# V of a sliding-window attention by dense products, one evacuation and SBUF-to-SBUF placement

## Chip, cores, metric

One core of one Trainium2 chip. The metric is device time in microseconds (us) of one execution. Kernels are compared only within the same rounds. All timed runs were fast but one, which is named.

## The reference

```python
h = layernorm(x) * (1 + ca) + sa            # x: 2048 x 512; ca, sa, ga, ... from c @ w_mod
q, k, v = split(h @ wqkv)                   # 32 heads of 16
scores = q k^T / 4, masked to 0 <= i - j < 256
x = x + ga * (softmax(scores) @ v @ wo)
h = layernorm(x) * (1 + cb) + sb
x = x + gb * (gelu(h^T @ w1 + b1) @ w2 + b2)^T   # token MLP, F = 1792
```

## The kernel before

The program is a list of about 1,380 small operations (`op`). `ORDER` says in which sequence they are put on the engines' instruction lists. It also names the engine where there is a choice: D for VectorE, A for ScalarE, P for GpSimd. Tokens are worked in four groups of 512, each of four blocks of 128 tokens. The attention runs in 75 chunks, E0 to E74. Each chunk has scores (S, TensorE into PSUM), two exponentials on ScalarE, a mask product, and products with V (AV, into `pxy`).

```python
def run_order(ops):
    for word in ORDER.split():        # "359D": operation 359, on VectorE
        n = int(word.rstrip("ADP")); o = ops[n]
        if any(d.n in left for d in o.deps): raise RuntimeError(o.name)
        left.discard(n); o.emit(...)
```

The V part of a block: 32-column tiles of TensorE put the tokens of the two 64-token halves where `VT` wants them. Two half-height casts bring them there. `VT` keeps zero columns beside every head, 16 columns of V and 16 of zeros, so it is cleared once.

```python
VT = [kvpool.tile([P, 8, DH, 2 * DH], BF, ...) for r in range(3)]   # group G uses VT[G % 3]
vt_zero = [[op("vz", ... memset(VT[r][:, 2*n : 2*n+2, :, :], 0.0)) for n in range(4)] for r in range(3)]

def v(tb, pos):                              # one block of 128 tokens
    for i in range(2):                       # two halves of 64 tokens
        for dc in range(ND):
            for q in range(4):
                te.matmul(pv[32*q : 32*(q+1), i, :], lhsT=h1T[:, dc, tok], rhs=wv[:, dc, q // 2, :, :],
                          tile_position=(0, 32 * q), ...)
    def e_ve(e, par):
        rows = slice(KB * par, KB * (par + 1))
        copy(e, VT[r3][rows, 2*tb : 2*tb+2, :, par*DH : (par+1)*DH], pv[rows, ...])
    bs = [op("ve", {"ACT": .53, "DVE": .62}, ...) for par in range(2)]
    v_done[G, tb] = bs
```

The softmax here doesn't subtract the row's maximum and nothing guards it: scores larger than these inputs give would overflow.

## Time and profile before

| | before |
|---|---|
| time, median (range) | 268.49 us (267.96 to 268.76, 3 runs) |
| start of the profile to the first exponential (E0) | 15.68 us |
| E0 to E74 | 171.10 us, ScalarE's gaps over 0.12 us sum to 5.1 (the 5.2 of the prediction takes in those from 0.10 on) |
| E74 to the end | 80.00 us |
| VectorE busy | 205.0 us |

ScalarE's row of 75 pairs of exponentials sets the time up to E74, and TensorE's products with w1 and w2 set it from there on. So three numbers tell a run: when E0 starts, how long E0 to E74 takes, and the tail. The lines behind this are in the prediction.

### The profile page before, as it was taken

The page shows a single profiled execution, that of the slowest core. Times are in us where ns is not written, and L with a number is a line of the kernel's source. Part 1 is how long each engine was busy: PE and PEld are TensorE (multiplying, and loading weights), DVE is VectorE, ACT ScalarE, POOL GpSimd, SP SyncE. Part 2 cuts the span into 40 slices and gives each one's busy share as a digit, 9 for nine tenths or more (in the row PEclk, how much of TensorE's full clock was granted, in tenths as well). Part 3 has the DMA queues.
Part 4 walks back from the last instruction along what each step waited for, and adds up shares of the span by engine and source line. Part 5 has one row for each costly group of instructions (what it writes and reads, how often), then busy time and mean ns, then how long its engine had stood idle before and what let it go on. Part 6 is the DMA issues. An engine that isn't in the chain of part 4 may idle for free.

```text
span 266.8 us, 10593 instructions
## 1 busy us (share of the span) xinstructions
PE 249.1 (93%) x4737; PEld 136.2 (51%) x4737; DVE 205.0 (77%) x439; ACT 186.6 (70%) x281; POOL 70.4 (26%) x146
## 2 busy tenths in 40 slices
PE   7799999999998996978999999999999999999993
PEld 2477655755666653644454544444534444444441
DVE  7588988879958589999946999999998640263585
ACT  3289999999998999998999999999613850000000
POOL 8667500624460781324920012010000000000000
PEclk9999999999999999999999999999999999999999
DMA  7999100002300005000090220035599600011122
GB/s 208 322 349 232 4 2 5 6 2 84 81 5 2 6 5 157 5 2 4 14 301 8 84 79 4 2 81 150 133 397 416 249 1 2 0 59 60 42 79 79
DMA packets 31446, 24.81 MB, mean 93 GB/s; under 512 B 6056, under 2 KB 29608, under 8 KB 31400
## 3 DMA queue, kind: packets, MB, share of 16 engines
q1 hardware_dynamic: 31392, 24.13, 29.8%
q8 instruction: 37, 0.61, 1.0%
q14 instruction: 9, 0.07, 0.1%
q10 hardware_dynamic: 8, 0.00, 0.0%
HBM read 22.03 MB, written 2.10 MB: 90 GB/s over the span
## 4 chain that ended last, share of the span: by engine, by line
PE 69%; DVE 14%; ACT 7%; DMA 5%; SPq 2%; issue 2%; DVEq 0%; ACTq 0%
PE pu L193 33%; PE pxy L193 10%; PE pq L193 9%; PE psa L193 9%; ACT et L193 5%; PE pa L193 4%; PE pv L193 3%; DVE VT L193 3%; DMA w<-in_B_w_dram 3%; DVE et L193 2%; DMA x<-in_A_x_dram 2%; DVE st L193 2%; SPq L193 2%; PE ps_b L193 1%; DVE h1T L193 1%
## 5 line engine op out<-in xcount | busy, mean ns | idle before, releaser
L193 ACT ACTIVATE et<-psa 128x1536 bf16<-128x1536 f32 x75 | 109.2, 1456 | 5.6 <-PE psa L193 2.6
L193 PE MATMUL pu<-hb,w1p 128*128 128x512 bf16 x224 | 54.6, 380 | 1.2 <-DVE part L193 0.5
L193 PE MATMUL pu<-guT,w 128*128 128x512 bf16 x224 | 49.2, 379 | 0.0
L193 ACT ACTIVATE et<-psb 128x512 bf16<-128x512 f32 x75 | 44.8, 601 | 0.0
L193 PE MATMUL pxy<-et,VT 128*32 128x192 bf16 (+3 forms) x960 | 37.7, 234 | 1.0 <-DVE OT L193 0.6
L193 PE MATMUL pxy<-et,ones_bd 128*32 128x192 bf16 (+3 forms) x960 | 37.9, 233 | 0.0
L193 PE MATMUL pq<-h1T,wqkv 128*128 128x512 bf16 (+1 forms) x160 | 34.1, 338 | 2.5 <-DVE kb L193 1.1
L193 PEld LDWEIGHTS <-w 128*128 128x128 bf16 x224 | 21.9, 98 | 26.4
L193 PE MATMUL psa<-QT,KT 32*128 32x192 bf16 (+3 forms) x720 | 30.0, 231 | 4.2 <-ACT et L193 3.5
L193 PEld LDWEIGHTS <-w1p 128*128 128x128 bf16 x224 | 20.0, 98 | 26.5 <-issue 4.0
L193 POOL TENSOR_SCALAR KT<-kb,mask_par 128x512 bf16<-128x512 bf16 (+1 forms) x36 | 24.1, 679 | 34.7 <-DVE kb L193 18.3
L193 DVE SCALAR_TENSOR_TENSOR o<-pu,b2FM,bc_gb 128x512 f32<-128x512 f32 x16 | 11.7, 748 | 25.2 <-PE pu L193 25.2
L193 PE MATMUL psb<-QT,KT 32*128 32x192 bf16 (+3 forms) x240 | 29.4, 231 | 0.0
L193 PEld LDWEIGHTS <-KT 32*128 32x128 bf16 x960 | 15.1, 92 | 26.8 <-issue 25.3
L193 PEld LDWEIGHTS <-VT 128*32 128x32 bf16 x960 | 23.3, 96 | 10.2 <-issue 8.7
L193 DVE TENSOR_TENSOR et<-et,maskt 128x512 bf16<-128x512 bf16 (+2 forms) x56 | 24.9, 479 | 0.5 <-ACT et L193 0.4
L193 PEld LDWEIGHTS <-ones_bd 128*32 128x32 bf16 x960 | 23.0, 97 | 0.1
L193 DVE BATCH_NORM_STATS2 st<-x 128x6 f32<-128x512 bf16 x32 | 21.9, 684 | 1.5 <-DMA x<-in_A_x_dram 1.3
L193 DVE CAST VT<-pv 64x512 bf16<-64x512 f32 x30 | 20.5, 686 | 3.0 <-PE pv L193 2.1
L193 PEld LDWEIGHTS <-wqkv 128*128 128x128 bf16 x160 | 13.4, 97 | 14.3 <-issue 4.9
L193 DVE TENSOR_TENSOR OT<-pxy,lz 128x256 bf16<-128x256 f32 x32 | 13.3, 415 | 9.5 <-ACT lz L193 9.4
L193 POOL TENSOR_SCALAR xn<-x,nm,rs 128x512 bf16<-128x512 bf16 x13 | 10.8, 834 | 32.2 <-DVE nm L193 22.6
(93 smaller groups left out, 347.5 us busy)
## 6 DMA issues: line engine op xcount, KB each, us to landing
w1p<-in_B_w_dram SPq DMA_DIRECT2D x14, 512.0 KB, 5.2
w<-in_B_w_dram SPq DMA_DIRECT2D x14, 512.0 KB, 10.1
wmod<-in_w_mod_dram SPq DMA_DIRECT2D x6, 512.0 KB, 6.6
x<-in_A_x_dram SPq DMA_DIRECT2D x16, 128.0 KB, 5.5
out_dram<-otile SPq DMA_DIRECT2D x16, 128.0 KB, 1.7
wqkv<-in_A_wqkv_dram SPq DMA_DIRECT2D x2, 384.0 KB, 6.2
wqkv<-in_A_wqkv_dram SPq DMA_DIRECT2D x1, 512.0 KB, 5.9
wod<-in_A_wo_dram SPq DMA_DIRECT2D x1, 512.0 KB, 8.9
```

Source lines behind the costliest of these rows:

```text
L193: ins = call(*args, **kwargs)
```

## The change

Intent: TensorE's products of V for groups 1 to 3 become dense (4 products of 512 columns per block in place of 32 small ones). A block is evacuated by one full-height cast into a small tile `VN` that has the zero columns already. Four SBUF-to-SBUF transfers of 64 KB (64 rows of 1 KB) put it into `VT`. Group 0 keeps the old way. The whole `ORDER` is new as well. The diff cut to its core (new list, names, and parts for another setting cut):

```diff
+VN_BUFS = 2
+VN = [kvpool.tile([P, 2, D + DH], BF, name=f"VN{r}") for r in range(VN_BUFS)]
-vt_zero = ... for r in range(3)
+vt_zero = ... VT[0] only;  vn_zero = [op("vz", ... memset(VN[n][:], 0.0)) for n in range(VN_BUFS)]
 def v(tb, pos):
+    te.matmul(box["v", tb][:], lhsT=h1T[:, dc, tb*P : (tb+1)*P], rhs=wqkv[:, dc, 2*D : 3*D], ...)
+    vr = len(v_placed) % VN_BUFS
+    copy(e, VN[vr][:, :, 0:D] ..., box["v", tb][:] ...)
+    b = op("ve", {"ACT": .495, "DVE": .6}, e_ve,
+           deps=[halves[1]] + (v_placed[-VN_BUFS] if len(v_placed) >= VN_BUFS else [vn_zero[vr]]))
+    for i in range(2):
+        for par in range(2):
+            sp.dma_start(out=VT[r3][KB*par : KB*(par+1), 2*tb + i, :, :] ...,
+                         in_=VN[vr][...][KB*i : KB*(i+1), D*par : D*(par+1)])
+            placed.append(op("vp", {"SP": .4}, e_vp, deps=[b] + war))
+    v_placed.append(placed); v_done[G, tb] = placed
```

Each `vp` is a word of its own in `ORDER`, and SyncE issues its transfers strictly in the order of the list.

## The prediction

> **What bounds the kernel now.** I read the page first, then the groups of instructions with shapes kept apart, then busy time by stage, then the order in time of ScalarE. The page says TensorE 93% busy, but the kernel has two regimes and only one of them is TensorE's.
>
> ```profile
> PE 249.1 (93%) x4737; PEld 136.2 (51%) x4737; DVE 205.0 (77%) x439; ACT 186.6 (70%) x281; POOL 70.4 (26%) x146
> ACT  3289999999998999998999999999613850000000
> L193 ACT ACTIVATE et<-psa 128x1536 bf16<-128x1536 f32 x75 | 109.2, 1456 | 5.6 <-PE psa L193 2.6
> L193 ACT ACTIVATE et<-psb 128x512 bf16<-128x512 f32 x75 | 44.8, 601 | 0.0
> ```
>
> The second line is ScalarE's busy tenths in 40 slices of 6.67 us: nearly all nines from slice 4 to slice 28, then little. Those are the 75 chunks of the attention, each with two exponentials. By stage (columns: stretch, length, busy us of PE, weight loads, DVE, ACT, POOL, clock, DMA share, GB/s):
>
> ```profile
> 64.00:96.00 32.00, 29.83 (x970) 19.38 (x959) 23.66 (x53) 30.81 (x47) 14.68 (x21) 1.00 0.08 20
> 96.00:128.00 32.00, 26.96 (x746) 16.39 (x744) 30.70 (x65) 30.44 (x43) 12.26 (x19) 1.00 0.14 36
> 128.00:160.00 32.00, 31.79 (x644) 15.72 (x648) 25.10 (x56) 31.17 (x44) 7.72 (x8) 1.00 0.39 101
> 189.00:266.80 77.80, 72.31 (x388) 32.47 (x386) 46.00 (x81) 14.37 (x30) 0.00 (x0) 1.00 0.33 123
> ```
>
> ScalarE is busy 30.4 to 31.2 us of every 32; between 96 and 128 us VectorE is just as full (30.7) while TensorE falls to 27.0. The last 77.8 us belong to TensorE. In the ScalarE timeline the first exponential starts at 15.68 us and the last at 186.78. Adding every gap of more than 0.12 us in front of a ScalarE instruction in between gives 5.2 us, 18 gaps, the two largest here:
>
> ```profile
> 14.96 0.82 ACT L193 ACTIVATE kb<-pq 128x256 bf16<-128x256 f32 x2 [1.05 <-PE pq L193]
> 15.68 1.44 ACT L193 ACTIVATE et<-psa 128x1536 bf16<-128x1536 f32 x1
> ...
> 84.45 1.45 ACT L193 ACTIVATE et<-psa 128x1536 bf16<-128x1536 f32 x1 [0.78 <-PE psa L193]
> ```
>
> (The other is 1.00 us at 124.93, waiting for psb.) So a change that touches neither the exponentials nor the last stage can win the start before 15.68 us and those 5.2 us, no more.
>
> **What the Trainium skill says.** "VectorE: DVE Perf Modes", section "Why `tensor_reduce` can't reduce along partition axis": the engine streams along the free dimension, every partition being its own lane. Then 64 partitions cost what 128 do, and the trace agrees: the first two rows below, 64x512 at 686 ns and 128x512 at 681. "TensorEngine Tiling (Array Packing)", "PSUM Bottleneck": tiling speeds up TensorE but not the evacuation. V before is such a case: its 32-column tiles put both heads of a pair in the right place, at two half-height evacuations per block. "DMA: Bandwidth & Descriptors", "Anatomy of one DMA": about 2 us fixed per transfer, given there for GpSimd's path; the nearest here, 128 KB stores on SyncE's queue, land in a median of 1.7 us.
>
> **The change, part by part.** These are the rows it acts on, from the groups by shape:
>
> ```profile
> L193 DVE CAST VT<-pv 64x512 bf16<-64x512 f32 x30 | 20.5, 686 | 3.0 <-PE pv L193 2.1 <-ACT VT L193 0.4
> L193 DVE CAST kb<-pq 128x512 bf16<-128x512 f32 x11 | 7.5, 681 | 0.1
> L193 POOL MEMSET VT<- 128x1024 bf16 x7 | 6.7, 952 | 0.1
> L193 DVE MEMSET VT<- 128x512 uint32 x5 | 2.4, 485 | 0.3
> L193 PE MATMUL pv<-wqkv,h1T 128*32 128x256 bf16 x512 | 17.1, 273 | 1.0 <-issue 0.4 <-DVE VT L193 0.4
> ```
>
> *Evacuations.* Groups 1 to 3 have 12 token blocks. 24 casts of 0.686 us (16.5 us) become 12 of 128x512 at about 0.68 (8.2): VectorE gives up 8.3 us.
>
> *Memsets.* The built program has 4 memsets of VT instead of 12, and 2 of the new tile VN: VectorE 5 to 3 (1.0 us less), GpSimd 7 to 3 (3.8 less). GpSimd is 26% busy, so that half is worth nothing directly.
>
> *TensorE.* 384 matmuls of 32x256 become 48 of 128x512. By durations this looks like a gift; it is not. The chain of waits shows 32 of the tiled ones, one block, in 0.87 us where nothing disturbs them (43.06), and four 512-column products of Q or K in 0.86 to 0.97. Four tiles side by side take a quarter of the time each. I book 0, though 672 fewer instructions stand in its queue.
>
> *What the new order moves.* The whole order of the program is a list, and it is a new one. Counting both built programs: VectorE takes over xn (3 x 0.42), kb (2 x 0.40 and 1 x 0.68), part (0.68), h1T (0.53 - 0.40), and gives up QT (0.41), h (0.42) and some small ones. That is about 2.7 us back, so VectorE's net is 8.3 + 1.0 - 2.7 = 6.6 us less. ScalarE between the first and last exponential loses h1T (0.77), kb (0.62), part (about 0.6), and gains h1T (0.56), KT (0.47), QT (0.39), a second evacuation of the first group's V inside chunk 0 and a pair of small rs (0.5); it had two such evacuations before too. Minus 2.0 plus 1.9: no change. **ScalarE's floor in the attention stays where it was.**
>
> *Start.* Before, ScalarE copies two kb tiles (14.96 to 15.78) ahead of the first exponential, although the first scores left TensorE at 14.4. In the new order these copies are VectorE's and come after it. Nothing then stands between: 14.4 to 14.5, 1.2 us earlier. h1T also comes ahead of a statistics pass that waited for x until 9.70, some tenths more. But VectorE then has about 11.8 us of work over the first five chunks (summed from the durations above), against 11.6 us that those took before; part of the lead is lost. I book 0.9.
>
> *Gaps.* Inside the critical stretch of 96 to 128 us there are 12 VT casts, 8.0 us, of which about half go. The 1.00 us gap at 124.93 lies right behind two such casts and a kb (122.48 to 124.5), and TensorE's queue waited for VT casts 7 times for 3.2 us in all. A block's PSUM buffer is now held for one cast, not two. I book 2.2 of the 5.2 us.
>
> *Transfers.* 48 of 64 KB, 64 rows of 1 KB. At 0.45 us per issue (14 w2 issues took 11.75 us with waits, x issues 0.42 to 0.46) that is 22 us of SyncE, idle otherwise between 25 us and the w1 loads. A block needs an evacuation (0.7), up to four issues (1.8) and a landing (about 1.7): 4.2 us, or two chunks of 2.3. In the built order the blocks of groups 2 and 3 precede their first use by at least four chunks; the tightest are the last three of group 1, two chunks ahead. I book 0.3 of new waits.
>
> *Last stage.* The same products stand behind the last exponential in both orders: 96 + 8 + 224. At 0.2165 us (250 in 54.13) that is 71.0 of its 77.8 us. One w1 load now follows three w2 loads, but about 44 products (9.5 us) precede its use. I book 0.
>
> Sum: 268.5 - 0.9 - 2.2 + 0.3 = 265.7.
>
> **The rivals.** *VectorE was the bound, so its whole 6.6 us come off:* for it, 30.7 of 32 us at 96 to 128; against, ScalarE has 30.4 in the same stretch and lost 1.2 us there. With the earlier start as well, and every gap closed, 261.5 to 262.5. *The transfers become the wait:* two VN tiles only, and a VN may be overwritten only when its four transfers have landed; some stand in SyncE's queue behind a 512 KB w1 load that takes 5.2 us to land. A late VectorE cast holds up what follows on that engine. For it, one such re-use within a chunk of its last transfer in group 3; against, VectorE has slack now. 267 to 270. *TensorE gains from 672 fewer instructions:* the weight loads show 49.2 us of "issue", so perhaps the queue limits it; then the gaps close faster, 264. Against: TensorE's idle time is in ScalarE's shadow.
>
> **Range and chances.** Best case 261.5, worst plausible 270; the parts that I book are each uncertain by about 1 us, and three executions of one kernel lay within 0.8. 8 in 10: 262.9 to 268.3. Faster by over 2% means under 263.1, nearly all gaps closed: 0.11. Slower by over 2%: 0.02.
>
> **What would show it.** Right if: ScalarE's first exponential starts at 14.0 to 14.8 us and its gaps up to the last sum to 2 to 4 us; VectorE's busy time falls by 5 to 8 us; a V block takes about 0.87 us of TensorE; the last stage keeps 77 to 78.5 us. Wrong if pxy products or VN casts wait for DMA by over 1 us in all, if a VN cast takes much over 0.7 us, or if the last stage moves by over 1 us.

## The result, and the profile after

| | before | after |
|---|---|---|
| time, median (range) | 268.23 us (267.73 to 268.76, 4 runs) | 269.63 us (269.24 to 269.73, 4 runs) |
| ratio | | 1.0049, 95% interval 1.0025 to 1.0073 |
| E0 / E15 in the profile | 15.68 / 52.41 us | 13.76 / 52.00 us |
| E15 to E74 | 134.37 us | 136.04 us |
| E74 to the end | 80.00 us | 79.49 us |

A ratio is the mean time of one kernel's fast runs over that of the other's of the same rounds, so not quite the ratio of the medians quoted. Later the same changed kernel had ratios of 1.0078 and 1.0032. I use the mean of the three, 1.0053, or +1.4 us, where I had predicted -2.8.

The prediction's own sign of failure ("wrong if pxy products or VN casts wait for DMA by over 1 us in all") is there: casts alone waited 3.7 us.

VectorE's relief came out exactly, and the casts cost what was said. From the page of the changed kernel, and from its groups by shape (columns: busy us, mean ns of one, idle before them and what ended it):

```profile
PE 244.8 (92%) x4355; PEld 131.9 (49%) x4401; DVE 198.4 (74%) x429; ACT 186.1 (70%) x278; POOL 63.7 (24%) x141
...
VT<-VN SPq DMA_DIRECT2D x48, 64.0 KB, 3.1
```

```profile
L195 DVE CAST VN<-pv 128x512 bf16<-128x512 f32 x12 | 8.3, 688 | 7.8 <-DMA VT<-VN 3.7 <-PE pv L195 2.2 <-PE psb L195 1.8
```

VectorE is at 198.4 us against 205.0: 6.6 less, as predicted. But the 12 casts stood idle 7.8 us, half of it for the transfers, and a transfer lands in a median of 3.1 us. The stretches that the prediction showed:

```profile
64.00:96.00 32.00, 29.14 (x876) 18.40 (x879) 22.89 (x51) 30.87 (x47) 11.58 (x20) 1.00 0.24 57
96.00:128.00 32.00, 25.88 (x600) 14.02 (x595) 29.16 (x67) 30.04 (x43) 12.49 (x16) 1.00 0.47 122
128.00:160.00 32.00, 31.51 (x600) 15.82 (x605) 23.65 (x53) 30.65 (x42) 4.23 (x6) 1.00 0.14 37
189.00:267.50 78.50, 72.30 (x408) 32.92 (x399) 47.12 (x83) 15.64 (x33) 0.00 (x0) 1.00 0.35 128
```

Between 96 and 128 us VectorE gave up 1.5 us, and ScalarE is no fuller than before (30.04 against 30.44). The relief is there and does not reach the engine that bounds.

The start, in ScalarE's timeline of the changed kernel (start, us, then what ran; brackets: idle before, and releaser):

```profile
13.76 1.45 ACT L195 ACTIVATE et<-psa 128x1536 bf16<-128x1536 f32 x1
15.11 0.59 ACT L195 ACTIVATE et<-psb 128x512 bf16<-128x512 f32 x1
15.59 0.30 ACT L195 ACTIVATE rs<-mv,eps_t 128x2 f32<-128x2 f32 x1
15.91 0.20 ACT L195 ACTIVATE rs<-rs 128x2 f32<-128x2 f32 x1
16.73 1.07 ACT L195 ACTIVATE VT<-pv 64x512 bf16<-64x512 f32 x2 [0.61 <-DVE VT L195]
17.70 1.44 ACT L195 ACTIVATE et<-psa 128x1536 bf16<-128x1536 f32 x1
19.03 0.59 ACT L195 ACTIVATE et<-psb 128x512 bf16<-128x512 f32 x1
20.11 0.56 ACT L195 ACTIVATE h1T<-pt,modFM 128x256 bf16<-128x256 bf16 x1 [0.49 <-PE pt L195]
```

E0 starts 1.92 us earlier, but work that stood ahead of E0 now stands between the first exponentials. ScalarE's work ahead of E0 is 2.7 us against 4.4 (one load of 1.28 us at the very beginning, the same in both, is left out). E4 starts at 26.36 against 24.79, later than before.

What the transfers did, from the timeline of the same run (VectorE, TensorE and ScalarE):

```profile
59.13 0.69 DVE L195 CAST VN<-pv 128x512 bf16<-128x512 f32 x1 [2.38 <-DMA VT<-VN]
...
62.49 0.69 DVE L195 CAST VN<-pv 128x512 bf16<-128x512 f32 x1 [1.28 <-DMA VT<-VN]
...
97.73 0.69 DVE L195 CAST VN<-pv 128x512 bf16<-128x512 f32 x1 [1.79 <-PE psb L195]
...
98.47 1.02 PE L195 MATMUL pq<-h1T,wqkv 128*128 128x512 bf16 x4 [0.43 <-DVE VN L195]
...
100.72 0.21 PE L195 MATMUL pxy<-et,VT 128*32 128x64 bf16 x4 [0.90 <-DVE OT L195]
...
102.06 0.38 ACT L195 ACTIVATE lz<-pxy 128x256 f32<-128x256 f32 x1 [0.74 <-PE pxy L195]
```

Three casts waited until a `VN` was free. The third is put down to `psb`, but its last transfer had landed only at 97.43. Its lateness runs through Q's products and `pxy` to ScalarE: E36 to E37 took 3.25 us, where the same order takes 2.53 when nothing waits (e17) and the old one 2.01. These three casts suggested a first theory, which turned out to explain only a part.

### The profile page after: what moved, and what is told of

It reads as the page before. It is cut to its first block, busy times and chain, and to the rows that moved or that the text cites. A ratio compares the mean times of both kernels' runs of the same rounds, so it can differ in the third digit from the quotient of the medians.

```text
span 267.5 us, 9950 instructions
## 1 busy us (share of the span) xinstructions
PE 244.8 (92%) x4355; PEld 131.9 (49%) x4401; DVE 198.4 (74%) x429; ACT 186.1 (70%) x278; POOL 63.7 (24%) x141
## 4 chain that ended last, share of the span: by engine, by line
PE 63%; DVE 13%; ACT 10%; DMA 7%; SPq 4%; issue 2%; DVEq 0%; ACTq 0%
PE pu L195 33%; PE pxy L195 11%; ACT et L195 8%; PE psa L195 7%; PE pq L195 6%; SPq L195 4%; DMA VT<-VN 3%; PE pv L195 2%; DVE st L195 2%; DMA wqkv<-in_A_wqkv_dram 2%; PE pa L195 2%; DVE VN L195 2%; ACT lz L195 2%; DMA wmod<-in_w_mod_dram 2%; DVE OT L195 1%
## 5 line engine op out<-in xcount | busy, mean ns | idle before, releaser
L195 PE MATMUL pu<-hb,w1p 128*128 128x512 bf16 x212 | 52.7, 380 | 2.2 <-DMA w1p<-in_B_w_dram 0.9
L195 PE MATMUL pu<-guT,w 128*128 128x512 bf16 x219 | 48.6, 379 | 0.3
L195 ACT ACTIVATE et<-psb 128x512 bf16<-128x512 f32 x75 | 44.2, 595 | 0.0
L195 PE MATMUL pq<-h1T,wqkv 128*128 128x512 bf16 (+1 forms) x149 | 33.5, 335 | 3.3 <-DMA wqkv<-in_A_wqkv_dram 1.0
L195 POOL TENSOR_SCALAR KT<-kb,mask_par 128x512 bf16<-128x512 bf16 (+1 forms) x36 | 22.8, 643 | 45.6 <-DVE kb L195 45.4
L195 PEld LDWEIGHTS <-VT 128*32 128x32 bf16 x960 | 23.9, 96 | 13.5 <-issue 11.1
L195 DVE SCALAR_TENSOR_TENSOR o<-pu,b2FM,bc_gb 128x512 f32<-128x512 f32 x16 | 11.8, 747 | 25.0 <-PE pu L195 24.8
L195 PE MATMUL pv<-wqkv,h1T 128*32 128x256 bf16 (+1 forms) x170 | 16.2, 300 | 1.8 <-DVE kb L195 0.6
L195 PE MATMUL pa<-wod,OT 128*128 128x512 bf16 x58 | 15.8, 380 | 0.6 <-issue 0.5
```

Source lines behind the costliest of these rows:

```text
L195: ins = call(*args, **kwargs)
```

## The experiments

**Theories.** R: the re-use of two `VN` tiles, with w1 loads of 512 KB in front of the transfers, makes casts late (the second rival of my prediction). O: the new order in itself is worse, apart from V. D came last, once the others had failed: the transfers are issued late because of their place in the list. In the texts the ordinals count from 1, so "the step to the 38th exponential" is E36 to E37. Three of them (e1, e4, e9) call the same step by the 37th.

E15 is where the start is over. The last column is ScalarE's gaps over 0.12 us from E0 to E74. E0 varies by 2 us between runs of the same start. It moves with the first loads: in 11 of the 12 fast profiles with the new start E0 came 5.6 us behind the landing of the first wqkv load (8.14 us in the changed kernel, 8.88 in e17), and in four of the seven with the old start 6.9 us behind it (8.75 in the kernel before). So the E15-to-E74 column is the cleaner one.

| run | ratio to before | 95% interval | E0 | E15 | E15 to E74 | gaps |
|---|---|---|---|---|---|---|
| before | 1 | | 15.68 | 52.41 | 134.37 | 5.1 |
| after | 1.0049 | 1.0025 to 1.0073 | 13.76 | 52.00 | 136.04 | 7.7 |
| e11, after again | 1.0078 | 1.0051 to 1.0106 | 13.29 | 51.70 | 136.01 | 7.9 |
| e16, after again | 1.0032 | 1.0009 to 1.0055 | 13.35 | 51.74 | 136.42 | 7.9 |
| e1, three VN | 1.0044 | 1.0014 to 1.0074 | 14.65 | 54.17 | 135.30 | 8.2 |
| e4, w1 aside | 1.0019 | 0.9990 to 1.0049 | 13.85 | 52.10 | 135.14 | 6.9 |
| e6, and a V half moved | 1.0036 | 1.0008 to 1.0064 | 15.56 | 53.84 | 135.58 | 7.4 |
| e13, three VN and w1 aside | 1.0030 | 1.0007 to 1.0052 | 13.46 | 52.91 | 136.08 | 8.9 |
| e14, w1 by GpSimd | 1.0111 | 1.0083 to 1.0139 | (slow profile) | | | |
| e9, 32 transfers out | 1.0002 | 0.9978 to 1.0025 | 14.66 | 52.90 | 134.40 | 6.3 |
| **e17, transfers behind casts** | **0.9954** | 0.9923 to 0.9984 | 14.52 | 52.76 | 133.72 | 5.8 |
| e18, and w1 aside | 0.9956 | 0.9929 to 0.9984 | 13.89 | 52.13 | 133.66 | 5.8 |
| e3, old V, new order | 1.0158 | 1.0126 to 1.0191 | 13.65 | 51.77 | 139.20 | 10.8 |
| e2, new V, old order | 0.9967 | 0.9931 to 1.0002 | 16.85 | 53.13 | 134.46 | 4.9 |
| e12, e2 again | 1.0001 | 0.9982 to 1.0021 | 14.76 | 51.66 | 134.46 | 5.8 |
| e5, e2 and w1 early | 0.9979 | 0.9953 to 1.0006 | 14.96 | 52.47 | 133.79 | 5.6 |
| e15, e2 and w1 by GpSimd | 1.0168 | 1.0137 to 1.0198 | 16.77 | 52.99 | 138.07 | 8.5 |
| e10, e2, 32 transfers out | 0.9947 | 0.9931 to 0.9962 | 15.35 | 51.62 | 133.78 | 4.5 |
| e7, before and w1 early | 1.0033 | 1.0007 to 1.0060 | 14.68 | 52.05 | 135.48 | 7.2 |
| e8, new start, old rest | 1.0164 | 1.0142 to 1.0185 | 13.50 | 57.80 | 133.54 | 11.3 |

### First call: re-use, order, loads (e1 to e4)

e1, a third tile, slots given in the order of the casts:

```diff
-VN_BUFS = 2
+VN_BUFS = 3
-vr = len(v_placed) % VN_BUFS
+vr = V_RANK[len(v_placed)] % VN_BUFS      # V_RANK: rank of each block's cast in ORDER
```

> The changed kernel with three VN tiles in place of two, in its own order; so a cast waits for the transfers of the third block before it, not of the second. Theory R (re-use of VN: the casts wait for transfers, 5.5 us of VectorE's idle time, and the wait at 97.7 us costs ScalarE 1.2 us): the three waits of casts disappear, ScalarE's gaps fall from 7.7 to about 6.5 us, and the time falls 0.7 to 1.5 us below the changed kernel's. Theory O (the cost lies in the order, with more of VT's and K's work between the first exponentials and other pile-ups): the waits disappear too, but the time moves by less than 0.4 us. Theory T (the transfers' landing itself is late for the products that read VT): less than 0.4 us as well, and the loss at the 37th exponential stays.

Measured 1.0044: no gain in time. One cast of group 1 (at 64.89) still stood idle 1.67 us. But E15 to E74 is 0.9 us shorter than the changed kernel's 136.2 (the mean of its three profiles). E36 to E54 took 40.74 us, as in e17, against 41.4 to 41.7: behind E36 the third tile removed what the transfers cost. The gain was eaten in the start, where E7 to E8 took 3.75 us in place of 2.84. The third tile's memset had been put on GpSimd right behind another, and VectorE's `xn` beside the two took over twice its time. From e1's timeline, and then from the changed kernel's:

```profile
32.88 1.89 POOL L196 MEMSET VN<- 128x1056 bf16 x2
33.26 1.66 DVE L196 TENSOR_SCALAR xn<-x,mv,rs 128x512 bf16<-128x512 bf16 x1
```

```profile
31.62 0.98 POOL L195 MEMSET VN<- 128x1056 bf16 x1
32.00 0.74 DVE L195 TENSOR_SCALAR xn<-x,mv,rs 128x512 bf16<-128x512 bf16 x1
```

That the memset slowed `xn` is a reading of these lines; both runs with a third tile show it, and no run takes it apart. So theory R fell in its plain form, as the waits ahead of E36 stayed, but it holds for the part behind E36.

e2 puts the new V into the old list: the words of the old V stay, and each block's four transfers follow its cast. e3 puts the old V into the new list.

```diff
 e2: ORDER = before's list;  "ve ve" of a block  ->  "ve vp vp vp vp"
 e3: ORDER = after's list;   "ve ... vp ... vp"  ->  "ve ve", the memsets of VT[1], VT[2] added
```

> The changed kernel's V code (dense products, one cast, four transfers, two VN tiles) in the order of the kernel before, each block's transfers issued right behind its cast. Theory O: 1.0 us or more below the kernel before, since the V change alone takes 6 to 7 us off VectorE and the order before had gaps of only 5.2 us; first exponential at about 15 us. Theory R: as slow as the changed kernel or slower (0 to +2 us against the kernel before), with casts of VN waiting for transfers. If neither change of order nor re-use matters: within 0.3 us of the kernel before.

> The kernel before's V code (tiled products, two casts into VT, all memsets) in the changed kernel's order. It has no transfers, so no wait for them. Theory O: it is slower than the kernel before, by 1 us or more, because the order is the cost and VectorE has its 6.6 us back. Theory R: the start gained by the order (first exponential at about 13.8 us) is kept in part, and it is at or below the kernel before, 0 to -1 us.

e2 came to 0.9967 and, repeated, 1.0001. e3 came to 1.0158. As a square this looks like a clear verdict for O: the order costs 4 us with the old V and about 2 with the new. It is a trap, though. In e2 I had also moved the transfers, right behind the casts. And e3's list was made for a VectorE with 6.6 us less to do. Its VectorE was busy 207.2 us, and ScalarE's gaps rose to 10.8.

e4 takes the w1 loads out of the transfers' way:

```diff
 ORDER (SyncE): two w1 words to behind group 1's transfers, one between the batches of group 2,
                two behind group 2, two behind group 3
```

> The changed kernel with seven 512 KB loads of w1 moved in SyncE's order: two go ahead of group 2's V transfers, one into the middle between two batches of them, two behind the last of group 2 and two behind those of group 3, so that hardly any transfer of VT is issued while such a load is under way; nothing else moves. Theory R with the loads as the cause of the late landing: the transfers of groups 2 and 3 land in 2 to 3 us in place of 4 to 6, the wait of the cast at 97.7 us falls from 1.8 to under 0.5 us, the 37th exponential loses under 0.3 us in place of 1.2, and the time falls 0.7 to 1.5 us. Theory O: landings fall the same way, the time moves by less than 0.4 us.

1.0019: the step E36 to E37 fell to 2.54 us as R had it, and E15 to E74 is 0.9 us shorter. E36 to E54 took 40.73 us, so this edit removed the same waits as e1's.

### Second call: refining the order (e5 to e8)

> New V in the old order, as in the run before with 0.9967 of the kernel before, with five of the 512 KB w1 loads issued earlier in SyncE's order (one at about 66 us, two between the two batches of group 2's transfers, two behind the second batch), so none is first asked for while it is still in flight and few transfers sit behind one. Theory L (late loads, of w1 itself and of transfers behind them): the gaps of 0.99 us at the 55th exponential (TensorE waited inside a product with w1) and of 0.47 us at 108.8 us (pxy waited for VT) vanish, and the time falls 1.0 to 1.5 us further, to a ratio of 0.991 to 0.994. Rival: another wait takes their place, as TensorE and VectorE are as full as before: ratio 0.996 to 0.998.

> The changed kernel with the w1 loads aside, as in the run before with 1.0019, and one more move: the first half of a V product of group 3 goes behind the scores of the 45th chunk on TensorE's list, because there it waited 0.65 us for VectorE to empty a PSUM bank (K casts behind three mask products) and the scores behind it waited too. Theory O (the order put this half in front of the scores): the step from the 44th exponential to the 45th falls from 3.1 to 2.1 or 2.2 us and the time by 0.7 to 1.0 us, to a ratio of 0.998 to 0.999. Rival: VectorE is the limit in this stretch, and the wait turns up at the next chunk: the step falls, the one behind it grows, ratio 1.001 to 1.003.

> Control: the kernel before, unchanged but for the same five w1 loads issued earlier. It has no V transfers. If early loads help only through the transfers, it is the same as the kernel before within 0.3 us. If the loads themselves were late for the products with w1, its 1.0 us gap at 124.9 us or a part of it goes, and it is 0.5 to 1 us faster; then that part of what early loads give is no gain of the V change.

> The new order up to the 9th exponential, and behind that the order of the run with the old order and early w1 loads. It tells what the new start alone is worth. My prediction had a gain of 0.9 us for it. Theory P (the new order starts the exponentials 1.9 us earlier only by putting ScalarE's own work of the start, some 3 us, between the first of them): within 0.4 us of the run with old order and early loads. If the start is a real gain: 0.7 to 1.2 us below it. First exponential at about 13.8 us in both cases[...].

The edits are in the list alone:

```diff
 e5, e7: five w1 words forward: to E21, E28 and E31, two behind group 2's second batch of V
 e6 (on e4):  -... v:840 F43 S44 ... v:841 ...      +... F43 S44 v:840 ... v:841 ...
 e8: the new list up to E8, behind it e5's list without the words that had been used
```

e5: 0.9979. The gap of 0.99 us at E54 went, as theory L had it, but a new one of 1.20 us came at 26.8 and one of 0.76 at 93.6. e7, the control, was not helped (1.0033). So early loads showed no gain in themselves. Ahead of all these gaps, the one at E54 included, stand stalls of TensorE that no instruction released (0.97 us in e2, 1.02 and 0.63 in e5, and three in e7's profile, 1.9 us in all; see the last section). Theory L did not mean those, so e5 and e7 do not measure it cleanly.

e6: E43 to E44 fell from 3.11 to 2.39 us, but E44 to E47 grew from 6.12 to 6.81. E43 to E47 is 9.20 against 9.23 us, so the wait moved and nothing was won: the rival was right.

e8 is spoilt at its seam, where 3.2 us of ScalarE's time are lost at 41.7 us. Only what lies ahead of the seam counts: E7 at 33.75 us, with E0 at 13.50. Old starts with E0 at 14.68 to 16.85 had E7 at 32.62 to 34.12. The earlier E0 had won nothing by E7.

### Third call: what the transfers cost in all (e9 to e12)

```diff
 def e_vp(e, i=i, par=par):
+    if G >= 2: return                       # 32 of the 48 transfers left out
-lhsT=VT[r][...]
+lhsT=VT[r % 2][...]                          # groups 2 and 3 read what is there: wrong on purpose
```

> The changed kernel without the 32 transfers of groups 2 and 3: their products read VT as groups 0 and 1 left it, so the result is wrong on purpose; all products, casts and the order stay. It bounds what these transfers cost the changed kernel in any way (casts that wait, late VT, w1 loads and transfers in each other's way). Theory R: 0.8 to 1.5 us below the changed kernel of the same rounds (1.0049 of before, so 0.9995 to 1.002), with the 37th exponential's step at 2.5 us in place of 3.25. Theory O: the rest of the excess, at least half of it, stays, as the order keeps its own waits (1.6 us of gaps in the first four chunks, 0.6 us at the 45th exponential, 0.5 us at the 55th).

> New V in the old order without the 32 transfers of groups 2 and 3 (wrong on purpose in the same way). In that order no cast of VN waited for a transfer, so theory R expects nothing: within 0.4 us of the same kernel with them (0.9967 of before). If it is 0.8 us or more faster, the transfers cost something that the waits don't show, for instance by delaying loads or the fetch of instructions.

> The changed kernel itself, for a comparison in the same rounds as the three beside it: 1.003 to 1.006 of the kernel before. The step to the 38th exponential should again be near 3.2 us, with the first exponential anywhere from 13.7 to 15.6 us.

> New V in the old order again, to firm up a ratio whose interval touched 1: 0.995 to 0.999 of the kernel before if the first result holds; 1.000 to 1.002 if that was luck. Under theory O it lies 0.6 to 1.0% below the changed kernel of the same rounds.

In the same rounds the changed kernel had 1.0078 and lost 0.76% of that without the transfers, 2.0 us. New V in the old order went from 1.0001 to 0.9947, 1.5 us. (At its tolerance the comparison with the reference doesn't see the wrong V.) My prediction had 0.3 us for all 48. And e11 told something else: the long step from E36 to E37, on which theory R was built, wasn't there again (2.53 us). The largest loss had appeared earlier instead. From e11's timeline:

```profile
83.49 0.10 PEld L195 LDWEIGHTS <-VT 128*32 128x32 bf16 x4 [1.16 <-DMA VT<-VN]
...
83.49 0.29 PE L195 MATMUL pxy<-et,VT 128*32 128x256 bf16 x4 [0.88 <-DMA VT<-VN]
...
84.40 1.45 ACT L195 ACTIVATE et<-psa 128x1536 bf16<-128x1536 f32 x1 [0.87 <-PE psb L195]
```

`pxy` waits 0.88 us for a transfer of VT, the scores behind it wait too, and ScalarE loses 0.87 us. Which wait shows differs from run to run; that some wait for VT shows does not.

### Fourth call: through what? (e13 to e16)

> The changed kernel with three VN tiles and with the seven w1 loads moved out of the transfers' way. If re-use and loads together make the transfers' cost, it comes to within 0.4 us of the changed kernel without the 32 transfers, 1.5 to 2.3 us below the changed kernel of the same rounds. If latency and traffic as such cost it (c), it lies 0 to 0.7 us below, like the single changes.

> The changed kernel with the first seven w1 loads issued by GpSimd, so that SyncE issues only transfers there; order as it is. If the transfers were late because they stood behind a load in one queue, they land in 2 to 3 us again and the time falls 0.8 to 1.5 us below the changed kernel of the same rounds. If the load delays them wherever it was issued, because both share the DMA engines, they stay at 4 to 6 us while one is in flight, and the time moves by less than 0.4 us, or rises if issuing costs GpSimd time that its masks of K need.

> New V in the old order, with the first seven w1 loads issued by GpSimd. As above: if the queue is the cause, the wait of pxy for VT at 108 us (0.4 to 0.5 us) goes and the time falls 0.4 to 1.0 us below the 0.9967 and 1.0001 of before that this kernel had with loads on SyncE; if the shared DMA engines are, it stays within 0.4 us of them.

> The changed kernel in the same rounds, as the yardstick for e13 and e14: 1.004 to 1.008 of the kernel before.

```diff
 e13: e1 and e4 together
 e14, e15:  -sp.dma_start(out=t[:], in_=w1_v[...])   +po.dma_start(...)      # first seven w1 loads
```

e13: 1.0030 beside the changed kernel's 1.0032 of the same rounds. By time, re-use and loads together explain nothing of it. The trace shows more: E36 to E54 took 40.74 us as in e1 and e4, 0.8 us less than in the changed kernel, so either edit removes that part, and both together remove it only once. Three losses hide it: e1's in the start (E7 to E8 took 3.76 us), a stall of 0.42 us at 186.1, and the largest gap, 1.14 us at 85.7, which is again at the place of e11's and which neither tiles nor loads had cured. e14 and e15 are slower by 0.8% and about 1.8% (e15's profile has a stall of 2.0 us at 142.4, so not all of this need be GpSimd's issuing). In e15 a transfer issued at 102.02 landed at 107.16, 5.1 us later, with loads in flight that GpSimd had issued. The queue is thus not what delays a transfer behind a load. The Trainium skill says the same in "DMA: Bandwidth & Descriptors", section "Issuing engines are not separate DMA queues": such transfers "interleave with each other, regardless of the engine that started them". One profile of e14 fell in a state with a clock of 0.56 and 401 us; it is not used.

### Fifth call: the place in the list (e17, e18)

So I asked where the transfers stand. In the changed kernel's list the last V block of group 1 (its cast is word 361, its transfers are 362 to 365) reads:

```
... 360 396 282 361D 397 369 283 558P 370 277 426 363 ...          cast and one transfer: at E19
... 588 451 572D 590 452 464 309 365 461 589 573 465 591 463 301P 574 362 617 364 ...    the rest: E26 to E27
```

Three of the four transfers stand seven or eight chunks behind their cast, between those of the next group's first block (588 to 591). The first product that reads them comes at E28, one chunk later. The others of group 1 are interleaved in pairs of blocks, so that a `VN` comes free only when the last of four is through. That is what made the casts at 59.13 and 62.49 wait.

e17 issues each block's four transfers right behind its cast and changes nothing else in the list. VN slots go by the order of the casts, as in e1. This second edit could not be tested alone with two tiles: the program refuses it in the changed kernel's list, where cast 368 stands ahead of transfer 350 of the tile that it would take. e1 and e13 had it, with a third tile. e18 also moves six w1 loads.

```diff
-... 361D 397 369 283 558P 370 277 426 363 ... 365 ... 362 ... 364 ...
+... 361D 362 363 364 365 397 283 558P 277 426 ...
-vr = len(v_placed) % VN_BUFS
+vr = V_RANK[len(v_placed)] % VN_BUFS
```

> The changed kernel in its own order, but with each block's four transfers issued right behind its cast (two VN tiles, taken in the order of the casts). Theory D (the list issues three transfers of group 1's last block too late): the wait of pxy at 83.5 us and ScalarE's gap at 84.4 us go, the stretch from the 28th to the 37th exponential falls from 20.7 to 21.1 us to 20.0 to 20.3 us (20.03 without the transfers), and the time falls about 1 us, to a ratio of 1.000 to 1.003 where the changed kernel had 1.0049, 1.0078 and 1.0032. Theory C (latency and traffic as such): the stretch stays above 20.6 us and the ratio within 1.003 to 1.008.

> The same with six of the 512 KB w1 loads moved between the blocks' transfers, so none stands in front of a transfer. Theory D with late loads on top: transfers of groups 2 and 3 land in 2 to 3 us, the step to the 38th exponential stays at 2.54 us, and the ratio comes to that of the changed kernel without 32 transfers, 0.998 to 1.002. If loads don't matter once the transfers are issued in time: the same as the run beside it within 0.1%.

0.9954 and 0.9956, better than theory D itself had forecast. The stretch E27 to E36 took 20.03 us in both, as without transfers (e9: 20.03), where the changed kernel had 20.71 to 21.10. The rest came from places that D had not counted (below). E15 to E74 is 133.7 us against the changed kernel's 136.0 to 136.4. e17's VectorE, for the same casts as above:

```profile
58.23 0.69 DVE L196 CAST VN<-pv 128x512 bf16<-128x512 f32 x1 [0.73 <-PE psb L196]
...
62.52 0.69 DVE L196 CAST VN<-pv 128x512 bf16<-128x512 f32 x1 [0.72 <-PE pv L196]
```

And from the waits of the whole run, all those of casts into VN (us in total, times, longest):

```profile
DVE VN L196 <- PE pv L196: 2.1, 3, 0.7
...
DVE VN L196 <- PE psb L196: 0.7, 1, 0.7
```

No cast, product or weight load waits for a transfer any more, with two tiles and with the w1 loads' words where they were (the transfers that now come earlier do get ahead of some of them). Transfers still land in a median of 2.7 us in e17 (2.1 in e18): their landing time isn't what mattered, but when they were issued. e17 is, with e18, the fastest correct kernel, 267.25 us against 268.37 of the kernel before in the same rounds. It beats both kernels, if by under 2%.

## Why the prediction was wrong, point by point

- **VectorE -6.6 us: right.** 205.0 to 198.4, and one cast of 128x512 took 688 ns as against the 680 booked.
- **TensorE, no gain: right.** A dense block took 0.96 us where nothing disturbs it (112.28 to 113.24 in e2), against 0.87 of the tiled one.
- **Last stage, 0: nearly.** From E74 to the end it took 79.5 us in every run with the new order and 80.0 with the old, so 0.5 us better. I did not look for the cause.
- **Start -0.9 us: wrong, 0.** E0 came even earlier than predicted (13.76, where "14.0 to 14.8" was said). But over the nine profiles with the new start and two tiles E15 lies at 52.33 us on average, and over the seven with the old start at 52.33; counted from the landing of the first wqkv load it is 43.95 against 44.01. "Part of the lead is lost" should have read "all". In the profiles of before and after, E0 to E15 took 36.73 and 38.24 us. Of these 1.5 us, ScalarE's gaps are 1.2 (2.56 against 1.37, most of it in the first four chunks) and its other work beside the exponentials 0.3 (8.64 against 8.30). The prediction had set 11.8 us of VectorE's work against the 11.6 us of the first five chunks; these took 15.1.
- **Gaps -2.2 us: mis-sized.** With the transfers issued in time (e17) E15 to E74 is 0.65 us shorter than before, and so it is in the old order with most of them left out (e10, 0.6). That, and not 2.2, is what was measured once nothing else stood in the way. How much of it is VectorE's relief is not shown: the one profile of before has a stall of 0.44 us at 82.40 in this stretch, e10 one of 0.83 (see the last section). e6 shows one case of why the relief is worth so little: a wait removed at one chunk turned up at the next.
- **Transfers +0.3 us: the step that failed.** E15 to E74 in the changed kernel is 136.2 us on average of three profiles, and 133.7 in e17: 2.4 us. By time it is 1.0053 less 0.9954, 2.7 us. My text had seen the place ("the tightest are the last three of group 1, two chunks ahead") and costed it by a block's evacuation, issues and landing, 4.2 us against two chunks of 2.3. In the list three of those transfers stand where SyncE reaches them one chunk ahead. Nothing of the 4.2 us was hidden by the seven chunks that had gone by since their cast. The 4.2 itself was nearly right: in e17 cast to last landing took 4.5 us (95.78 to 100.31), though transfers that follow each other were issued 0.64 us apart (median, in every run that has them), not 0.45.

  Against e17, the changed kernel's 2.4 us lie in these places (means of its three profiles). E27 to E36, where `pxy` waits for late data: 0.9 us. E20 to E27, behind the last cast of group 1 (62.49), which waits for its tile: 0.5. E36 to E54, the part that e1 and e4 also removed: 0.8. Behind E60, where no transfer is under way: 0.3, which is not theirs. So 2.1 us are the transfers' cost by the traces.

The sum with the measured sizes: start 0, gaps -0.65, last stage -0.5, transfers +2.4, so +1.3 us. The mean of the three ratios says +1.4.

My rival "the transfers become the wait" had the right time, 267 to 270, and a part of the mechanism. Two tiles and w1 loads account for 0.8 us of the 2.1 (e1, e4, e13), and both were harmless when the transfers were issued in time (e17 has two tiles, and e18's loads moved aside add nothing to it). A late transfer made the tiles scarce; the tiles did not make the transfers late.

Theory O fell for the part beyond the start: e17, in the new order, is as fast from E15 to E74 as the old order at its best (133.7 against 133.8 in e5 and e10). It does not clear the order altogether: e5 and e10 each contain a stall in this stretch behind which a chunk took 0.9 to 1.0 us longer, and e17 has none. Two things stay open. e3, the old V in the new list, is 4 us slower than before; that a list fits only the work it was made for is my reading, no run takes it apart. And e12 was 1.5 us slower than e10, though its transfers stand behind their casts. The traces show 0.5 us of it as theirs, a `pxy` that waited for VT behind w1 loads near 107 us; another 1.0 us lies at E4 to E5 and E53 to E54, behind stalls of TensorE (0.48 us at 25.3, and 1.48 at 137.8 against e10's 0.83).

## What to carry to other kernels

When a copy becomes a transfer, look up where it is issued and not only when its data are wanted. A queue that works in order keeps a transfer back as long as the list does, and a wait for the landing then shows up at the reader, at the re-used buffer, or somewhere else in each run. So issue it right behind its producer, and test that before buying buffers or moving other loads. Look at where a run loses before calling a theory dead by its time: e1 had gained behind E36 what it lost in the start. And a 2x2 of "change" and "order" is only clean if nothing rides along: my e2 had carried the cure in it without my seeing it, and the square pointed at the order.

## What the Trainium skill lacked or had wrong

- "DMA: Bandwidth & Descriptors", "Anatomy of one DMA": about 2 us fixed, given for GpSimd's path. SyncE's 64 KB transfers land in 1.9 to 2.0 us when alone, so it holds there too. What is lacking is the landing with a 512 KB load in flight: up to 6.1 us in the changed kernel. Transfers issued 0.7 to 2.6 us behind the load of 121.41 landed 4.2 to 5.8 us later, just behind the load (127.62).
- "DMA: Bandwidth & Descriptors", "Rules for kernel authors": "Issue the DMA early, do compute, wait on its semaphore late". Right, and here most of the result: issued behind the cast 0.9954, issued up to eight chunks later 1.0053. The page doesn't say that a late issue also costs the source's buffer (casts idle 2.4 and 1.3 us).
- "Runtime: NRT & Kernel Launch", "Instruction fetch mechanics": crossing a 16 KiB block is there said to be "mostly hidden". In these runs TensorE has stalls of 0.35 to 2.0 us that no instruction released, one of them (e2, at the word "issue") here:

```profile
139.09 0.82 PE L196 MATMUL pu<-hb,w1p 128*128 128x512 bf16 x3 [0.97 <-issue]
...
141.14 1.45 ACT L196 ACTIVATE et<-psa 128x1536 bf16<-128x1536 f32 x1 [0.99 <-PE psb L196]
```

  Behind the start, the fast profiles have 13 such stalls of over 0.3 us (before, e2, e5, e7, e8, e10, e12, e13, e15). In all 13 a 16 KB packet of the instruction queue had ended 1.36 to 1.60 us before TensorE went on, and in 11 data of other transfers were moving meanwhile. That they are late fetches is an inference; no run tested it.
